# Pooled attention and top-1 experts on one core: a second block of the first expert between attention and the expert loop

## The chip, the cores and the metric

The kernel runs on one core of one Trainium2 chip. The metric is device time in microseconds (us), the median of several runs of one program. Engines are named as in the profile: PE (matrix multiply), PEld (its weight loads), DVE (vector), ACT (scalar), POOL (GpSimd), SP (queue of DMAs). `PEq`, `SPq` and the like are the engines' sequencers.

## The reference

```python
# attention, batch 8, heads 8, seq 576, head_dim 64: keys and values are means over 8 rows
scores = scale * np.matmul(q, k_p.transpose(0, 1, 3, 2))
attn = softmax(scores);  x = (attn @ v_p) as [4608, 512]
# experts: 8, each 512 -> 1024 -> 512; each token goes to the one with the largest logit
logits = x @ w_gate
expert_idx = np.argmax(logits, axis=1)
gate_w = softmax(logits)[np.arange(N), expert_idx]
for e in range(E):
    h = np.maximum(x_sorted[lo:hi] @ w1[e], 0.0)
    y_sorted[lo:hi] = h @ w2[e]
return gate_w[:, None] * y
```

How many tokens an expert gets depends on the data. With the inputs that the reference draws first, the experts 0 to 7 get 1018, 55, 333, 239, 827, 724, 24 and 1388 of the 4608 tokens. Of the first 2304 tokens (batches 0 to 3), 1016 go to expert 0.

## The kernel before

**Attention** runs over 36 units of 128 tokens. Units form seven groups (`bounds`, sizes 6, 6, 6, 6, 6, 4, 2). At the end of a group `route` finds each token's expert and its place among that expert's tokens, and POOL scatters the rows (`scatter`, one indirect DMA per unit) into the DRAM tensor `xs`, which has one segment per expert. Small steps of a route (`fillers`) are spread over later units; what belongs to unit 28, 29 and so on is put there by `put`.

**An early block.** Expert 0 is computed first, in blocks of 256 tokens (`BLK`). After group 2, `early_pe` (line 719) counts whether expert 0 has 256 tokens already and sets the flag `okf`. At unit 28 POOL blanks the tile `xg` (`blank_x`), at unit 29 SP loads the first 256 rows of `xs` into it if the flag is set (`early_load`, line 913). At units 30 and 31 the tile is split into a high and a low half-precision part (`split_early`, on POOL) and turned by two DMA transposes (`turn`) into `xT`. Its first three up products (`UPAT`, of eight) run on PE in units 33 to 35.

**A block** is eight up products (`up`, lines 967 to 969: 12 matmuls each), `relu_hi` on ACT and `relu_lo` on DVE for each of four pairs, and the down products (`finish`, line 1039: 12 matmuls for each half of the hidden columns and each of the two tiles of 128 tokens, 48 in all). `take` (ACT) scales a result, `give` (POOL) scatters it to the output. In a half block (at most 128 tokens) the up products have 128 columns and there are 24 down matmuls.

**Between attention and the loop** (lines 1046 to 1234) stand, in program order: the last group's route steps (`front`, `rest`); ups 3 to 7 of the early block, with `counted` (line 1057: count per expert, ranks, padding) behind the fifth up, `ended` (line 1089: end of each expert's blocks, the last rank chain, all pending scatters, three padding scatters, and `table`, 27 small DVE steps that make the loop's table) behind the sixth, and `tables` (line 1140: a PE transpose of the table and a DVE copy) behind the eighth; then the four `relu_lo`; then the early block's 48 downs. Behind them the x tiles of the loop's first blocks are loaded by the table (`load_x`), split and turned.

**The loop** (line 1260 on) runs T times, T read from the table. Iteration t does block t's ups and downs from `xT`; `arrive` (DVE) copies the next block's transposed tile from `xTs` to `xT`, `split_x` splits the one after it, `trans` sends it through the DMA transpose, `load_x` loads the one after that. In an expert's first block `part` splits the next expert's weights (ACT and DVE), and `wwhole` then loads whole experts' weights, two at the first iteration. Each engine works in program order; SP's queue issues its DMAs in program order too.

Of the kernel before, what the change touches and what calls it, by code (L numbers as in the profile page):

```python
# [32 lines left out]
def kernel(  # L33
# [171 lines left out]
    for e in range(E):  # L205
# [15 lines left out]
    xg, xg2 = (VB[i].rearrange("p y c s x -> p (y c s x)").bitcast(F32)[:, 0:2 * XW]  # L221
               .rearrange("p (j x) -> p j x", j=2) for i in (2, 0))
# [388 lines left out]
    def route(gidx):  # L611
# [107 lines left out]
        def early_pe():  # L719
            pm = psA.tile([128, 512], F32, name="pq", bufs=2)  # L720
            nc.tensor.matmul(pm[:, 0:1], ones, Z["c16"][:, 0:1], start=True, stop=True)
            V.tensor_scalar(okf, pm[:, 0:1], 256.0, None, op0=OP.is_ge)
# [190 lines left out]
    def early_load():  # L913
        assert KVS.pop("early") and not any(g < EARLY for g, _, _ in pend)
        KVS["ok"] = nc.values_load(oki[0:1, 0:1], engines=[ENG.SP], min_val=0, max_val=1)
        with tc.If(KVS["ok"] > 0):
            ld = nc.sync.dma_start(xg, xs[0:BLK, :].rearrange("(j p) x -> p j x", p=128))
        for o in scat[bounds[EARLY][0]:]:
            tc.declare_no_dep(ld.ins, o.ins, reason="rows of other tokens")
        soon.append(ld)  # L920

    put(28, "sp", blank_x, xg)
    put(29, "sp", early_load)
# [123 lines left out]
    rest = [f for _, _, f in fillers]  # L1047
    for x in range(max(len(front), len(rest))):
# [97 lines left out]
    for f in range(FC):  # L1146
        if f >= len(UPAT):
            up(0, f, BLK)
        if f + 1 == 5:
            counted()  # L1150
        if f + 1 == 6:
            ended()
        if f + 1 == 8:
            tables()
        if f in (1, 3):
            relu_hi(f // 2)
    for k in (2, 3):
        relu_hi(k)
    for k in range(4):
        relu_lo(k)  # L1160
    views = [x.rearrange("p a b c -> p (a b c)") for x in qt] + [x.rearrange("p c x -> p (c x)")[:, 0:2048] for x in kv[1:]]
    views = [x.bitcast(F16) for x in views]
    W1[1] = [x.rearrange("p (c f) -> p c f", c=DC) for x in views[:2]]
    W2[1] = [x.rearrange("p (c f) -> p c f", c=FC) for x in views[2:]]
    pY.append(psA.tile([128, 512], F32, name="pq", bufs=2))
    for j, half in ((1, 0), (1, 1), (0, 0), (0, 1)):
        finish(0, j, half)
# [26 lines left out]
    xh2 = kv[1].rearrange("p c x -> p (c x)")[:, 0:1024].bitcast(F16).rearrange("p (j a x) -> p j a x", j=2, a=2)  # L1194
    blank_x(xg2)
    load_x(0)
    load_x(1, xg2)
    wlate(1)
    for j in range(2):
        x, h, l = row(xg[:, j:j + 1]), col(xh[:, j:j + 1, 0]), col(xh[:, j:j + 1, 1])  # L1200
        nc.scalar.activation(h, x, AF.Copy)
# [113 lines left out]
```

## Time and profile before

| | us |
|---|---|
| Median of 3 runs | 645.25 |
| Lowest and highest | 642.09, 645.43 |
| The profiled execution's own time | 646.38 |
| Its span, first to last instruction | 644.4 |
| PE busy | 579.3 |

The profiled execution has 2.0 us around its span. Attention ends near 200 us, the loop's first up product starts at 228.70 us and the last instruction of PE ends near 636 us. PE idles little in the loop; rows with an idle time in brackets show where it does.

### The profile page before, as it was taken

The page shows a single profiled execution, that of the slowest core. Times are in us where ns is not written, and L with a number is a line of the kernel's source. Part 1 is how long each engine was busy: PE and PEld are TensorE (multiplying, and loading weights), DVE is VectorE, ACT ScalarE, POOL GpSimd, SP SyncE. Part 2 cuts the span into 40 slices and gives each one's busy share as a digit, 9 for nine tenths or more (in the row PEclk, how much of TensorE's full clock was granted, in tenths as well). Part 3 has the DMA queues.
Part 4 walks back from the last instruction along what each step waited for, and adds up shares of the span by engine and source line. Part 5 has one row for each costly group of instructions (what it writes and reads, how often), then busy time and mean ns, then how long its engine had stood idle before and what let it go on. Part 6 is the DMA issues. An engine that isn't in the chain of part 4 may idle for free. (4 is left out here: it accounts for less than half of the span.)

```text
span 644.4 us, 15871 instructions
## 1 busy us (share of the span) xinstructions
PE 579.3 (90%) x4694; PEld 422.3 (66%) x4695; DVE 316.9 (49%) x619; ACT 286.8 (45%) x635; POOL 276.4 (43%) x532
## 2 busy tenths in 40 slices
PE   6888898787977698998899999999999989999994
PEld 5777788676865275675566667766667666677662
DVE  7577678886675417221773755122722262221212
ACT  2576688677651226222672753122722352221222
POOL 6799689998684323112314123222121232012212
PEclk9798999899899699999899999999999989999998
DMA  8997789858476565963689497533231333213200
GB/s 244 290 287 222 231 231 311 266 176 248 168 214 232 192 120 152 384 164 85 168 247 327 108 321 251 153 102 77 42 81 53 96 72 102 49 57 79 65 16 30
DMA packets 104203, 108.15 MB, mean 168 GB/s; under 512 B 62310, under 2 KB 72550, under 8 KB 104168
## 3 DMA queue, kind: packets, MB, share of 16 engines
q1 hardware_dynamic: 97528, 86.72, 47.9%
q0 software_dynamic: 6640, 20.99, 8.8%
q8 instruction: 19, 0.31, 0.2%
q14 instruction: 16, 0.13, 0.1%
HBM read 72.99 MB, written 23.37 MB: 150 GB/s over the span
## 5 line engine op out<-in xcount | busy, mean ns | idle before, releaser
L1039 PEld LDWEIGHTS <-bd 128*128 128x128 f16 x936 | 91.6, 99 | 110.1 <-issue 3.6
L1224 POOL TENSOR_TENSOR spacer<-ql,iG 1x1 f32<-1x1 f32 x44 | 23.8, 540 | 218.9 <-ACT ql L1220 218.0
L1033 DVE SCALAR_TENSOR_TENSOR bd<-ps,bd 128x512 f16<-128x512 f32 x44 | 30.2, 690 | 151.3 <-ACT bd L1029 149.5
L1033 DVE SCALAR_TENSOR_TENSOR bd<-pp,bd 128x512 f16<-128x512 f32 x44 | 30.3, 691 | 100.7 <-ACT bd L1029 100.7
L513 ACT ACTIVATE both<-ps,nmx 128x72 f32<-128x72 f32 x288 | 69.0, 330 | 23.9 <-DVE nmx L506 23.3
L1029 ACT ACTIVATE bd<-pp 128x512 f16<-128x512 f32 x44 | 26.2, 597 | 116.8 <-PE pp L969 74.3
L1039 PE MATMUL po<-w,bd 128*128 128x512 f16 x264 | 59.1, 379 | 0.8 <-ACT bd L1029 0.8
L1029 ACT ACTIVATE bd<-ps 128x512 f16<-128x512 f32 x44 | 26.1, 597 | 74.8 <-PE L967 46.1
L1039 PE MATMUL po<-kv,bd 128*128 128x512 f16 x264 | 58.9, 379 | 0.3 <-ACT bd L1029 0.3
L1225 POOL DMA_INDIRECT out_dram<-ql,iG x44 | 43.8, 995 | 21.5 <-issue 20.2
L496 PE MATMUL ps<-bd,qT 128*128 128x144 f32 x256 | 47.0, 310 | 3.5 <-DMA bd<-bd 1.9
L967 PE MATMUL ps<-kv,qt 128*128 128x256 f16 (+1 forms) x176 | 45.7, 267 | 4.9 <-issue 3.2
L1039 PE MATMUL pq<-kv,bd 128*128 128x512 f16 x216 | 48.1, 379 | 0.0
L969 PE MATMUL ps<-kv,qt 128*128 128x256 f16 (+1 forms) x176 | 45.6, 267 | 1.9 <-DVE qt L118 1.9
L967 PE MATMUL ps<-kv,w 128*128 128x256 f16 (+1 forms) x176 | 43.8, 262 | 3.1 <-DVE kv L118 2.8
L969 PE MATMUL ps<-kv,w 128*128 128x256 f16 (+1 forms) x176 | 43.8, 262 | 2.5 <-DVE w L118 2.5
L968 PE MATMUL ps<-kv,qt 128*128 128x256 f16 (+1 forms) x176 | 45.7, 267 | 0.0
L1039 PE MATMUL pq<-w,bd 128*128 128x512 f16 x192 | 45.3, 395 | 0.3 <-remote 0.3
L554 PE MATMUL po<-vb,ph 128*128 128x146 f16 (+2 forms) x384 | 33.4, 234 | 12.6 <-DMA vb<-vc 7.0
L969 PE MATMUL pp<-kv,qt 128*128 128x256 f16 (+1 forms) x176 | 44.7, 263 | 0.0
L968 PE MATMUL pp<-kv,qt 128*128 128x256 f16 (+1 forms) x176 | 44.7, 263 | 0.0
L967 PE MATMUL pp<-kv,qt 128*128 128x256 f16 (+1 forms) x176 | 44.7, 263 | 0.0
(236 smaller groups left out, 1335.8 us busy)
## 6 DMA issues: line engine op xcount, KB each, us to landing
both<-in_moe_w_dram SPq DMA_DIRECT2D x6, 2048.0 KB, 11.7
st<-in_moe_w_dram SPq DMA_DIRECT2D x6, 2048.0 KB
vb<-x_by_expert SPq DMA_DIRECT2D x17, 578.0 KB
st<-in_moe_w_dram SPq DMA_DIRECT2D x8, 1024.0 KB
kv<-in_k_dram SPq DMA_DIRECT2D x7, 1024.0 KB
kv<-in_v_dram SPq DMA_DIRECT2D x7, 1024.0 KB
qt<-in_q_dram SPq DMA_DIRECT2D x6, 1024.0 KB
qt<-in_q_dram SPq DMA_DIRECT2D x4, 512.0 KB
```

Of the source, the lines that this page charges most:

```text
L496: nc.tensor.matmul(ps[:, x * 2 * KP:(x + 1) * 2 * KP], t[:, h, :], BD[b % 3][:, :, h, :], start=True, stop=True)
L513: nc.scalar.activation(p[:, h * KP:(h + 1) * KP], ps[:, x * KP:(x + 1) * KP], AF.Exp, bias=nmx[:, x:x + 1], scale=-1.0)
L554: nc.tensor.matmul(po[:, half, cols], a[:, c * 128:(c + 1) * 128], VB[b % 3][:, y, c, sl, 0:CW], start=st, stop=False, skip_group_check=True)
L967: nc.tensor.matmul(dst, wh, xT[:, d, 0:n], start=(d == 0), stop=False)
L968: nc.tensor.matmul(dst, wh, xT[:, DC + d, 0:n], start=False, stop=False)
L969: nc.tensor.matmul(dst, wl, xT[:, d, 0:n], start=False, stop=(d == DC - 1))
L1029: nc.scalar.activation(hT[0][:, 2 * k:2 * k + 2, :].rearrange("p f t -> p (f t)"), pH[k], AF.Relu)
L1033: V.scalar_tensor_tensor(l, pH[k], 0.0, h, op0=OP.max, op1=OP.subtract)
L1039: nc.tensor.matmul(y, hT[x][:, f, 128 * j:128 * j + 128], W2[s][z][:, f, :], start=(half == x == z == f == 0), stop=(half == z == 1 and f ...
L1224: nc.gpsimd.tensor_tensor(spacer[:, 0:1], ys[j][0:1, 0:1], iG[0:1, j:j + 1].bitcast(F32), op=OP.add)
L1225: st = nc.gpsimd.indirect_dma_start(out=out, out_offset=bass.IndirectOffsetOnAxis(ap=iG[:, j:j + 1], axis=0), in_=ys[j], in_offset=None, b ...
```

## The change

The second block of expert 0 is also computed between attention and the loop. `early_pe` sets the flag to 1 or 2 (256 or 512 tokens); the second early load fills a second tile `xg2`, which now lies in `kv[1]`, as does its split copy `xh2`, and is blanked at unit 28 as well. The loop then has as many blocks fewer as the flag says. `relu_hi(0)` and `relu_lo(0)` go ahead of the last group's route steps, the other relus follow their ups; `counted` stands behind the sixth up; the second tile's split and transpose and then `ended` stand behind the eighth; the first block's downs come in the order of tiles 0, 1; `arrive` for the second block stands among them, and `tables` behind them. Then come the second block's ups, relus and downs, with the loads, splits and transposes for the loop's first two blocks between them.

```diff
@@ -218,8 +218,10 @@
     hT = [x.rearrange("p (f t) -> p f t", f=FC) for x in bd[0:2]]
     xh = bd[2].rearrange("p (j a x) -> p j a x", j=2, a=2)
     ys = [x.rearrange("p h d -> p (h d)") for x in ql]
-    xg, xg2 = (VB[i].rearrange("p y c s x -> p (y c s x)").bitcast(F32)[:, 0:2 * XW]
-               .rearrange("p (j x) -> p j x", j=2) for i in (2, 0))
+    xg, xg2 = (x.rearrange("p (j x) -> p j x", j=2)
+               for x in (VB[2].rearrange("p y c s x -> p (y c s x)").bitcast(F32)[:, 0:2 * XW],
+                         kv[1].rearrange("p c x -> p (c x)")[:, 1024:1024 + 2 * XW]))
+    xh2 = kv[1].rearrange("p c x -> p (c x)")[:, 0:1024].bitcast(F16).rearrange("p (j a x) -> p j a x", j=2, a=2)
 
     def blank_x(x):
         nc.gpsimd.memset(x, 0.0)
@@ -719,7 +721,8 @@
         def early_pe():
             pm = psA.tile([128, 512], F32, name="pq", bufs=2)
             nc.tensor.matmul(pm[:, 0:1], ones, Z["c16"][:, 0:1], start=True, stop=True)
-            V.tensor_scalar(okf, pm[:, 0:1], 256.0, None, op0=OP.is_ge)
+            V.tensor_scalar(okf, pm[:, 0:1], float(BLK), None, op0=OP.is_ge)
+            V.scalar_tensor_tensor(okf, pm[:, 0:1], 2.0 * BLK, okf, op0=OP.is_ge, op1=OP.add)
 
         def early_int():
             V.tensor_copy(oki, okf[0:1, :])
@@ -912,14 +915,16 @@
 
     def early_load():
         assert KVS.pop("early") and not any(g < EARLY for g, _, _ in pend)
-        KVS["ok"] = nc.values_load(oki[0:1, 0:1], engines=[ENG.SP], min_val=0, max_val=1)
-        with tc.If(KVS["ok"] > 0):
-            ld = nc.sync.dma_start(xg, xs[0:BLK, :].rearrange("(j p) x -> p j x", p=128))
-        for o in scat[bounds[EARLY][0]:]:
-            tc.declare_no_dep(ld.ins, o.ins, reason="rows of other tokens")
-        soon.append(ld)
+        ok = nc.values_load(oki[0:1, 0:1], engines=[ENG.SP], min_val=0, max_val=2)
+        for n, x in enumerate((xg, xg2)):
+            with tc.If(ok > n):
+                ld = nc.sync.dma_start(x, xs[n * BLK:(n + 1) * BLK, :].rearrange("(j p) x -> p j x", p=128))
+            for o in scat[bounds[EARLY][0]:]:
+                tc.declare_no_dep(ld.ins, o.ins, reason="rows of other tokens")
+            soon.append(ld)
 
     put(28, "sp", blank_x, xg)
+    put(28, "sp", blank_x, xg2)
     put(29, "sp", early_load)
 
     def first_block():
@@ -1045,6 +1050,8 @@
     pH += [pp[:, 0:512], pp[:, 512:1024]]
     pY = [psA.tile([128, 2, 512], F32, name="po")[:, 0, :]]
     rest = [f for _, _, f in fillers]
+    relu_hi(0)
+    relu_lo(0)
     for x in range(max(len(front), len(rest))):
         for f in (front[x:x + 1] + rest[x:x + 1]):
             f()
@@ -1146,25 +1153,30 @@
     for f in range(FC):
         if f >= len(UPAT):
             up(0, f, BLK)
-        if f + 1 == 5:
+        if f == 3:
+            relu_hi(1)
+            relu_lo(1)
+        if f == 5:
             counted()
-        if f + 1 == 6:
-            ended()
-        if f + 1 == 8:
-            tables()
-        if f in (1, 3):
-            relu_hi(f // 2)
     for k in (2, 3):
         relu_hi(k)
-    for k in range(4):
         relu_lo(k)
+    split_x(xg2, xh2)
+    keep_ids(xg2)
+    move_ids()
+    trans(xh2)
+    ended()
     views = [x.rearrange("p a b c -> p (a b c)") for x in qt] + [x.rearrange("p c x -> p (c x)")[:, 0:2048] for x in kv[1:]]
     views = [x.bitcast(F16) for x in views]
     W1[1] = [x.rearrange("p (c f) -> p c f", c=DC) for x in views[:2]]
     W2[1] = [x.rearrange("p (c f) -> p c f", c=FC) for x in views[2:]]
+    finish(0, 0, 0)
+    finish(0, 0, 1)
     pY.append(psA.tile([128, 512], F32, name="pq", bufs=2))
-    for j, half in ((1, 0), (1, 1), (0, 0), (0, 1)):
-        finish(0, j, half)
+    finish(0, 1, 0)
+    arrive()
+    finish(0, 1, 1)
+    tables()
 
     def entry(kind, t, engines, lo, hi):
         ap = tabs[kind:kind + 1, t:t + 1] if isinstance(t, int) else tabs[kind:kind + 1, ds(t, 1)]
@@ -1190,29 +1202,6 @@
                 part(64, 64, x[64:128, 0])
                 with tc.If(many > 1):
                     part(128, 64, x[0:64, 1])
-
-    xh2 = kv[1].rearrange("p c x -> p (c x)")[:, 0:1024].bitcast(F16).rearrange("p (j a x) -> p j a x", j=2, a=2)
-    blank_x(xg2)
-    load_x(0)
-    load_x(1, xg2)
-    wlate(1)
-    for j in range(2):
-        x, h, l = row(xg[:, j:j + 1]), col(xh[:, j:j + 1, 0]), col(xh[:, j:j + 1, 1])
-        nc.scalar.activation(h, x, AF.Copy)
-        V.tensor_tensor(l, x, h, op=OP.subtract)
-    keep_ids()
-    move_ids()
-    turn()
-    load_x(2)
-    split_x(xg2, xh2)
-    keep_ids(xg2)
-    trans(xh2)
-    with tc.If(nc.values_load(tab[0:1, 1:2], engines=[ENG.Activation, ENG.DVE, ENG.SP], min_val=0, max_val=1) > 0):
-        for j in range(8):
-            wsplit(1, j)
-        wwhole(2, 1)
-        wwhole(3, 0)
-    T = nc.values_load(tab[0:1, 0:1], min_val=1, max_val=TMAX)
 
     given = []
 
@@ -1229,10 +1218,42 @@
             tc.declare_no_dep(st.ins, o.ins, reason="rows of other tokens")
         given.append(st)
 
+    take(0)
     take(1)
     give(1)
+    give(0)
+    take_ids()
+    load_x(0)
+    load_x(1, xg2)
+    for h in range(2):
+        for f in range(4 * h, 4 * h + 4):
+            up(0, f, BLK)
+        for k in (2 * h, 2 * h + 1):
+            relu_hi(k)
+            relu_lo(k)
+    split_x()
+    keep_ids()
+    move_ids()
+    trans()
+    for half in range(2):
+        finish(0, 1, half)
+    arrive()
+    load_x(2)
+    split_x(xg2, xh2)
+    keep_ids(xg2)
+    trans(xh2)
+    take(1)
+    give(1)
+    for half in range(2):
+        finish(0, 0, half)
     take(0)
     give(0)
+    with tc.If(nc.values_load(tab[0:1, 1:2], engines=[ENG.Activation, ENG.DVE, ENG.SP], min_val=0, max_val=2) > 0):
+        for j in range(8):
+            wsplit(1, j)
+        wwhole(2, 1)
+        wwhole(3, 0)
+    T = nc.values_load(tab[0:1, 0:1], min_val=1, max_val=TMAX)
 
     def part(s, en):
         with tc.If(en > 0):
```

## Rows read from the trace of the kernel before

**Rows 1.** The page, busy time by engine: each engine's busy time, share of the span and instructions.

```profile
PE 579.3 (90%) x4694; PEld 422.3 (66%) x4695; DVE 316.9 (49%) x619; ACT 286.8 (45%) x635; POOL 276.4 (43%) x532
```

**Rows 2.** Busy time in stretches around the hand-over from attention to the loop (all of core 0): the stretch, its length, busy us of each engine with its instructions, the clock granted to TensorE as a share of full speed, the DMA share, GB/s.

```profile
207.82:214.81 6.99, 0.01 (x2) 0.03 (x1) 3.05 (x27) 0.00 (x0) 6.06 (x11) 0.69 0.77 290
214.81:223.40 8.59, 8.26 (x26) 3.19 (x27) 3.88 (x7) 2.24 (x4) 0.38 (x3) 0.66 0.44 142
228.70:239.18 10.48, 10.48 (x96) 9.40 (x97) 1.38 (x2) 1.81 (x3) 2.80 (x11) 1.00 0.88 160
239.19:249.70 10.51, 10.51 (x50) 4.61 (x47) 8.63 (x9) 9.27 (x11) 0.20 (x1) 1.00 0.29 54
249.70:252.52 2.82, 0.01 (x1) 0.03 (x1) 2.82 (x4) 1.67 (x3) 1.58 (x1) 1.00 0.27 61
252.52:273.35 20.83, 20.83 (x144) 14.10 (x145) 5.25 (x7) 4.10 (x6) 5.92 (x16) 1.00 0.99 370
```

**Rows 3.** The timeline of PE at the hand-over: start us, us, engine, line, operation, out<-in, count, and in brackets the idle time before it and what ended it.

```profile
199.54 0.27 PE L967 MATMUL ps<-kv,w 128*128 128x256 f16 x1
...
203.42 0.18 PE L1059 MATMUL pq<-c,ones 128*128 128x8 f16 x1 [1.10 <-DVE c L1052]
...
204.84 0.34 PE L1093 MATMUL pq<-lt,ones 128*128 128x8 f16 x8
...
214.81 0.37 PE L1142 MATMUL pq<-ident,tf 128*8 128x128 f32 x1 [6.99 <-DVE tab L1138]
215.51 7.89 PE L1039 MATMUL pq<-w,bd 128*128 128x512 f16 x24 [0.33 <-remote]
...
228.70 0.28 PE L967 MATMUL ps<-kv,w 128*128 128x256 f16 x1
```

**Rows 4.** The groups of instructions with shapes apart, first of the three lines of the up product into PSUM tile ps: the operands (the name after the comma is the up weights' tile: w for slot 0, which the even experts use, qt for slot 1), the shape, the count, busy us and mean ns. A full block (256 tokens) has 16 such instructions of 128x256, a half block (128 tokens) 16 of 128x128.

```profile
L967 PE MATMUL ps<-kv,qt 128*128 128x256 f16 x144 | 40.0, 278 | 2.3 <-DVEq L1238 0.8 <-ACT qt L116 0.8 <-issue 0.7
...
L967 PE MATMUL ps<-kv,w 128*128 128x256 f16 x128 | 35.6, 278 | 3.1 <-DVE kv L118 2.8 <-DVE bd L899 0.2
...
L967 PE MATMUL ps<-kv,w 128*128 128x128 f16 x48 | 8.2, 219 | 0.0
...
L967 PE MATMUL ps<-kv,qt 128*128 128x128 f16 x32 | 5.7, 219 | 2.5 <-issue 2.5
```

**Rows 5.** The timeline of DVE at the hand-over, columns as in group 3: the first and the last of the last group's rank chain, the first and the last instruction of the table, then one `relu_lo`, one `arrive` and one low half of `split_x` from the loop's first block.

```profile
204.45 0.17 DVE L674 TENSOR_TENSOR rt<-pq,roh 128x16 f32<-128x16 f32 x1
...
205.97 0.17 DVE L697 RECIPROCAL both<-res 128x2 f32<-128x2 f32 x1
209.00 0.22 DVE L1112 TENSOR_SCALAR tf<-pq,tv 128x1 f32<-128x1 f32 x1 [2.85 <-PE pp L969]
...
213.49 0.14 DVE L1138 TENSOR_TENSOR tab<-pq,okf 1x1 int32<-1x1 f32 x1
...
240.25 0.69 DVE L1033 SCALAR_TENSOR_TENSOR bd<-pp,bd 128x512 f16<-128x512 f32 x1 [4.55 <-ACT bd L1029]
...
242.37 0.68 DVE L910 COPY kv<-kv 128x2048 f16<-128x2048 f16 x1
242.97 1.22 DVE L899 TENSOR_TENSOR bd<-vb,bd 128x1024 f16<-128x1024 f32 x1
```

**Rows 6.** The timeline of POOL at the hand-over, columns as in group 3: the first and the last of the six row scatters that are pending at the end of attention (three more, of padding, follow them).

```profile
202.42 0.97 POOL L702 DMA_INDIRECT x_by_expert<-both,rpos  x1 [7.10 <-DVE pq L640]
...
208.80 0.97 POOL L702 DMA_INDIRECT x_by_expert<-both,rpos  x1 [0.21 <-issue]
```

**Rows 7.** The timeline near the end of attention, columns as in group 3: POOL's blank of the first early x tile, SP's early load and the eight moves behind it and the transposes of the first block, then PE where it waits for the last move, and the first early up.

```profile
168.83 1.09 POOL L225 MEMSET vb<- 128x1156 f32 x1
...
171.70 0.37 SPq L917 DMA_DIRECT2D vb<-x_by_expert  x1
172.31 7.80 SPq L1014 DMA_DIRECT2D vb<-vc  x8
180.59 2.77 SPq L903 DMA_TRANSPOSE kv<-bd  x2
...
181.44 0.58 PE L554 MATMUL po<-vb,ph 128*128 128x73 f16 x7 [0.66 <-DMA vb<-vc]
...
187.15 0.27 PE L967 MATMUL ps<-kv,w 128*128 128x256 f16 x1
```

**Rows 8.** The timeline of SP's queue at the start of the loop, columns as in group 3: the two loads of x tiles as soon as the table is there, and the first transpose that the loop waits for.

```profile
217.64 2.81 SPq L1179 DMA_DIRECT2D vb<-x_by_expert  x2
...
228.86 4.02 SPq L906 DMA_TRANSPOSE kv<-kv  x1
```

**Rows 9.** DMA issues with their median time from issue to landing: first two rows over the whole execution, then two of the stretch 252 to 276 us, in which the next two experts' weights are loaded.

```profile
out_dram<-ql,iG POOLq DMA_INDIRECT x44, 3.0
...
kv<-bd SPq DMA_TRANSPOSE x23, 4.3
...
out_dram<-ql,iG POOLq DMA_INDIRECT x4, 7.2
kv<-bd SPq DMA_TRANSPOSE x1, 13.9
```

**Rows 10.** Where the loop first enters the body for half blocks of slot 1: PE's timeline, columns as in group 3, and the instruction queue in the stretch 293 to 298 us (packets, MB, share of 16 engines).

```profile
296.81 0.22 PE L967 MATMUL ps<-kv,qt 128*128 128x128 f16 x1 [2.45 <-issue]
...
q8 instruction: 1, 0.02, 1.1%
```

## The prediction

> **What bounds the kernel now.** I read the busy times first [rows 1]: PE is busy for 579.3 of 644.4 us. So I asked where PE is not busy, by stretches and by its timeline around the hand-over from attention to the loop. In the loop a full block takes PE 20.83 us and fills it: 10.48 us of ups and, from the difference, 10.35 us of downs, at the full clock [rows 2]. The loop is bound by PE; a block taken out of it is worth 20.83 us, and the same block put anywhere else costs 20.83 us of PE again. The change can win only where PE idles or is clocked low. The hand-over is such a place: PE's last up ends at 207.82 us, and it then waits 6.99 us for the end of `table` on DVE, only to transpose it [rows 3]; in that stretch PE is busy for 0.01 us [rows 2]. The downs behind it start at a granted clock of 0.66 on the mean of 8.59 us [rows 2], after the idle stretch, so that 48 of them take 228.70 - 215.51 = 13.19 us [rows 3] where the loop needs 10.35: 2.84 us lost.
>
> **Does the block leave the loop?** Only if the flag is 2, that is, if expert 0 has 512 of the first 2304 tokens. Counting the reference's argmax on the inputs as drawn gives 1016. The trace agrees with these inputs: 16 first-line ups make a block, so 144 + 128 instructions of 128x256 are 9 + 8 = 17 full blocks, and 48 + 32 of 128x128 are 3 + 2 = 5 half ones [rows 4]; the counts per expert give 4 full blocks for expert 0, and 17 full and 5 half in all. So T falls from 21 to 20, and the block that goes is a full one. The loop from its first up to the end of the span is 644.40 - 228.70 = 415.70 us before; one block less makes 394.87. The 2.82 us behind the first iteration, where PE waits for the split of the next expert's weights [rows 2], stays: that iteration keeps this work.
>
> **PE's new order, and the sum.** I start at 199.54, the fourth up, the same instruction in both kernels [rows 3].
> - Three ups at 10.48 / 8 = 1.31: 3.93.
> - Wait for the count. Before, PE waits 1.10 behind two ups [rows 3]. One more up stands ahead now (1.31 less waiting), but `relu_lo(0)`, 0.69 [rows 5], stands ahead of the DVE chain that makes the count's operand: 1.10 - 1.31 + 0.69 = 0.48.
> - Count, ranks and the eight small matmuls of `ended`: from the trace some 0.1 behind 203.42 and 0.2 behind 204.84 [rows 3]: 0.31. Their operand `lt` is on DVE by then.
> - Two ups, 2.62; the first block's downs at once, 10.35; the transpose of the table, 0.37 [rows 3], which now finds the table done.
> - The second block: 20.83.
>
> That is 38.89, so the loop starts at 238.43, and the span is 238.43 + 394.87 = 633.30: 11.10 us less, as the place lost 6.99 + 2.84 + 0.33 and part of the 1.10. This is the sum without any new wait.
>
> **What is added beside PE, and what hides it.**
> *Second early load and blank.* POOL's second blank, 1.09 and a small one [rows 7], stands ahead of the split of the first block and so of the transposes at 180.59. SP's second load stands ahead of the eight moves that PE waits for at 181.44, after which it was idle; the first load and its branch hold SP from 171.70 to 172.31, 0.61 us [rows 7]. Nothing hides that: the moves are issued one behind the other, and the last of them ends PE's wait. The first transposes start at 180.59 and the first early up at 187.15 [rows 7], 6.56 later; with 4.3 to landing and two of them issued in 2.77, the 1.2 us of POOL about uses up what is left over. The bounds are 0 (other engines set the pace after it) and 2.0 us (0.61, the 1.2 of POOL, and a wider branch); I take 0.8, nearest to the SP row.
> *The chain to the second block's `xT`.* All in DVE's order behind the eighth up, in the sum without shift at 206.9: `relu_hi(3)` on ACT (taken as 0.7, like the `relu_lo` of 0.69), the split's high half on ACT (taken as 1.2, like the low half) and its low half, 1.22, which ends near 210; then the rank chain, 205.97 + 0.17 - 204.45 = 1.69, the table, 213.49 + 0.14 - 209.00 = 4.63, and the copy `arrive`, 0.68 [rows 5]: 217.0. PE is done with the first downs and the table's transpose at 217.6. The slack is 0.6 us; a table that took as long as before hides just under the 10.35 us of downs, and without that cover it would cost the 6.99 again. The transpose has from 210 to 216.3 to land, 6.3 us, against a median of 4.3 [rows 9].
> *POOL.* `keep_ids(xg2)` waits for the split's end and stands ahead of the pending scatters, so these start near 210.5 and not at 202.42; six at (208.80 - 202.42) / 5 = 1.28 [rows 6] end at 218.2, with 3.0 to landing 221 (estimate by the other indirect DMA, [rows 9]). The loads of the loop's first tiles wait for them and for the table at 218: issued near 221, as 217.64 before [rows 8], landed by 225, and their first reader, `split_x`, comes behind the second block's ups at 228.1. 3 us of slack: no cost.
> *The transpose for the loop's first block* goes out near 231 and is needed at 238.4: 7.4 less 0.68 for the copy against 4.3 to landing, or some 6.3 where the issue itself takes 4.02 and not 2 [rows 8]. No cost. The flag's extra DVE step, the moved waits for the table's registers and `give` lie beside PE's work.
> I take 0.3 for the `xT` chain (0 to 2) and 0.5 for what the shorter run of expert 0 does to the next expert's start (0 to 3.4, third rival). Gain: 11.10 - 0.8 - 0.3 - 0.5 = 9.5 us. The profiled execution's own time, 646.38, becomes 636.9; it stands 1.1 above the median of the three runs, and the forecast for the median is 645.25 - 9.5 = 635.8.
>
> **A rule against it, twice.** The loads of two experts' weights make a transpose land after 13.9 us and an output scatter after 7.2 in place of 3.0 [rows 9]. The Trainium skill, "DMA: Bandwidth & Descriptors", section "Issuing engines are not separate DMA queues", says that DMAs from any engine end on the same 16 DMA engines and interleave. By that rule the new transpose, which now runs beside POOL's scatters, is late (second rival), and the rows above agree that traffic stretches it. At the first entry of the half body of slot 1 PE waits 2.45 us for nothing the profile shows, and one packet of the instruction queue falls into that stretch [rows 10]. The Trainium skill, "Runtime: NRT & Kernel Launch", section "Instruction fetch mechanics", says that a taken branch out of the fetched window has to fetch its code by DMA. By that rule the third rival is real.
>
> **The rivals.**
> 1. *Forecast*: PE runs through, 635.8. For it: every chain above fits under PE's work. Against it: the slack of the `xT` chain is under 1 us.
> 2. *The second block's transpose is late.* From a landing over 6.3 us PE waits at 217.6. At 9 it costs 2.7: 638.5. At the 13.9 of the weight loads [rows 9] it costs 7.6 and the low clock again, 2.84: no gain is left, 645 to 646. Against it: the scatters' stretch has a DMA share of 0.77 [rows 2], weight loads fill it.
> 3. *The next expert's start.* One block less lies between the loads of 8 MB of weights in the first iteration and expert 1's half block, which PE reaches 2 x 20.83 + 2.82 = 44.5 us after the loop's start in place of 65.3. The transposes and x loads queued behind the weights, and the entry of [rows 10], then fall into their end. If the 2.45 stretches as the output scatters do, 7.2 / 3.0 = 2.4 times, it costs 3.4: 638.7.
> 4. *The flag comes out as 1, not 2* (the change doesn't do what it says). Then the extra block works on a blank tile and the loop keeps 21 blocks: the loop starts at 238.43 + 1.6 in place of 228.70, 11.3 us slower: 656.6. It decides from the 512th token of expert 0 among the first 2304; 1016 speak against it.
>
> **How the numbers follow.** Chances: 1 has 0.66, 2 has 0.13 (most of it near 638.5), 3 has 0.14, 4 has 0.03, and 0.04 is for a long stall that I don't see, within or past 645. The range takes in the sum without new waits less what the runs scatter (645.25 - 11.1 = 634.2, lowest run 3.2 below its median; I go to 632.8) and, above, the attention tail at 2.0, 1.8 of `xT` and 3.4 of rival 3 together: 645.25 - 3.9 = 641.3; I go to 641.0. About 0.5%, 3.2 us, is what a measurement of this kernel can tell from no change. Faster than 642.0 are case 1, nearly all of 3 and most of 2: 0.88; within it the rest of 2 and of the last: 0.08; slower 0.04.
>
> **What would show it.** Right: PE without an idle gap over 1 us from the fourth up to the loop, its clock at 1.00 throughout, the 48 first downs in some 10.4 us, 20 `arrive` copies within the loop, the loop's first up near 239 to 240 us, and the span near 635. Wrong: a wait of PE for DVE's `arrive` before the second block's ups (rival 2), a wait over 3 us ahead of the 128x128 ups of slot 1 (rival 3), 21 loop blocks still (rival 4), or an attention that ends more than 2 us later.

## The result, and the profile after

The changed kernel is slower, not faster: 646.46 us median over 20 runs (642.8 to 651.7) against 644.21 over 20 runs of the kernel before on the same chip, ratio 1.0063, 95% interval [1.0038, 1.0088]. The ratio, here and below, leaves out the runs in a slower state that some executions fall into, so it is not the quotient of the medians, which is 1.0035 here. The forecast was a gain of 9.5 us. The profiled execution's own time is 645.5, its span 643.5; before these were 646.38 and 644.4. PE's work is the same, and its busy time rose by 3.6 us, which is the first sign of a lower clock in places. The page's busy time by engine:

```profile
PE 582.9 (91%) x4694; PEld 427.6 (66%) x4695; DVE 321.3 (50%) x620; ACT 286.0 (44%) x634; POOL 276.0 (43%) x532
```

The block did leave the loop. PE's timeline of the changed kernel at the hand-over (start us, us, engine, line, operation, out<-in, count, idle before it and what ended it), the rows that answer to [rows 3]: the fourth up, the matmuls behind the eighth, the first downs, the table's transpose, the second block's first up, the loop's first up, and last the half body's first entry, which answers to [rows 10]:

```profile
200.97 0.27 PE L972 MATMUL ps<-kv,w 128*128 128x256 f16 x1
...
208.10 0.34 PE L1100 MATMUL pq<-lt,ones 128*128 128x8 f16 x8
208.31 1.02 PE L1044 MATMUL po<-w,bd 128*128 128x512 f16 x4
...
222.06 0.27 PE L1149 MATMUL pq<-ident,tf 128*8 128x128 f32 x1 [3.23 <-DVE tab L1145]
222.57 0.35 PE L972 MATMUL ps<-kv,w 128*128 128x256 f16 x1 [0.24 <-DVE kv L913]
...
246.52 0.28 PE L972 MATMUL ps<-kv,w 128*128 128x256 f16 x1 [1.28 <-ACTq L1286]
...
297.66 0.24 PE L972 MATMUL ps<-kv,qt 128*128 128x128 f16 x1 [4.62 <-issue]
```

The first downs went as forecast: right behind the ups, done in 222.06 - 3.23 - 208.31 = 10.5 us. Then come three waits that the sum did not have: 3.23 for a table that is still late, 1.28 at the loop's entry where there was next to none before, and 4.62 at the half body's entry where it was 2.45 [rows 10]. The loop's first up comes at 246.52, not 238.43. The busy times by stretch (stretch, length, PE, PEld, DVE, ACT, POOL with their instructions, TensorE's granted clock, DMA share, GB/s) answer to [rows 2]:

```profile
208.31:222.06 13.75, 10.52 (x54) 4.63 (x51) 6.47 (x38) 3.51 (x5) 7.88 (x18) 1.00 0.64 189
222.06:234.50 12.44, 12.20 (x96) 10.10 (x97) 1.96 (x4) 1.19 (x2) 6.83 (x16) 0.86 0.78 234
234.50:246.52 12.02, 10.74 (x53) 4.80 (x50) 4.44 (x5) 4.47 (x6) 1.35 (x8) 1.00 0.29 59
246.52:270.37 23.85, 21.01 (x144) 13.95 (x145) 12.87 (x14) 12.11 (x15) 5.37 (x13) 1.00 0.38 92
```

The idle time ahead of the table's transpose is again followed by a lower granted clock: 0.86 on the mean of the second block's ups, which take some 12 us instead of 10.48.

**Why the table is late.** DVE's timeline of the changed kernel, from the second block's split through the last group's rank chain to the table's end (answers to [rows 5]):

```profile
211.24 1.23 DVE L902 TENSOR_TENSOR kv<-kv 128x1024 f16<-128x1024 f32 x1 [0.26 <-ACT kv L901]
212.38 0.17 DVE L676 TENSOR_TENSOR rt<-pq,roh 128x16 f32<-128x16 f32 x1
212.65 0.17 DVE L679 TENSOR_REDUCE rpf<-rt 128x2 f32<-128x16 f32 x1
218.22 0.17 DVE L696 CAST rpos<-rpf 128x2 int32<-128x2 f32 x1 [5.39 <-DMA x_by_expert<-both,rpos]
...
221.78 0.14 DVE L1145 TENSOR_TENSOR tab<-pq,okf 1x1 int32<-1x1 f32 x1
221.84 0.67 DVE L913 COPY kv<-kv 128x2048 f16<-128x2048 f16 x1
```

The chain stops in its third instruction. The cast writes the tile of positions `rpos`, which comes from a pool of two buffers; the one it gets was that of the last full group of six units, and the scatters of that group read it. They were expected to be long done. POOL's timeline shows why one was not (answers to [rows 6]):

```profile
197.30 0.97 POOL L704 DMA_INDIRECT x_by_expert<-both,rpos  x1 [0.22 <-issue]
198.29 0.20 POOL L881 TENSOR_TENSOR gC<-kv,zf 128x2 f32<-128x2 f32 x1
198.44 0.20 POOL L882 TENSOR_TENSOR iC<-kv,zi 128x2 int32<-128x2 int32 x1
212.61 0.20 POOL L886 TENSOR_TENSOR kv<-far,zi 128x2 int32<-128x2 int32 x1 [13.97 <-DVE rt L676]
...
213.38 0.98 POOL L704 DMA_INDIRECT x_by_expert<-both,rpos  x1 [0.26 <-issue]
```

Five of the six scatters are out by 198.3. The sixth stands in POOL's queue behind `keep_ids(xg2)`, whose last step overwrites the identity column of the second block's x tile and so has to wait 13.97 us until DVE has read that tile in the split (the split ends at 212.47; the row names the instruction right behind it). The sixth scatter goes out at 213.38, lands some 4.8 us later, and only then DVE may cast the positions. The table, which the prediction had done at 217.0 - 0.68 = 216.3 (217.8 on this execution's clock, whose fourth up is 1.43 later), is done at 221.92.

**Why the loop is entered late.** ACT's last scaling of outputs, `take(0)`, now belongs to the second block and runs behind its downs; ACT's arrival at the loop stands behind it, and so does the branch on the table with the loading of the loop's count, which the change put last:

```profile
240.23 0.69 ACT L1209 ACTIVATE ql<-pq,gB 128x512 f32<-128x512 f32 x1 [1.46 <-POOL iC L882]
245.27 0.69 ACT L1209 ACTIVATE ql<-po,gB 128x512 f32<-128x512 f32 x1 [4.36 <-PE po L1044]
```

PE's downs end at 245.24, the scaling at 245.96, and PE enters at 246.52.

**Why the half body is entered late.** SP's timeline: the loads of two experts' weights in the loop's first turn (8 MB), and the transpose behind them.

```profile
268.61 3.30 SPq L89 DMA_DIRECT2D both<-in_moe_w_dram  x2
272.76 6.42 SPq L89 DMA_DIRECT2D st<-in_moe_w_dram  x2
287.67 8.88 SPq L909 DMA_TRANSPOSE kv<-bd  x1
```

Before, the same loads were issued at 251.37 and 254.86. They belong to the loop's first turn, behind that turn's transpose; the first turn was the second block and is now the third, so they slid by 17 us on the clock, and by some 20 against the blocks. Two stretches ahead of the entry, columns as in the stretches above, show that they now reach it:

```profile
288.00:293.00 5.00, 5.00 (x24) 2.06 (x22) 0.00 (x0) 0.69 (x1) 1.38 (x3) 1.00 1.04 392
293.00:298.00 5.00, 0.38 (x4) 0.23 (x3) 0.00 (x0) 0.69 (x1) 1.81 (x6) 0.97 1.20 215
```

In the kernel before the DMA engines were idle at 286 to 290 us; here they are full (shares over 1 are overlapping packets) until PE starts. The packet of the instruction queue that belongs to the entry starts at 294.64, 1.6 us after PE went idle; before, it started at 294.12, 0.2 us ahead of PE's idle time. From the packet's start to PE's it is 2.6 to 3.1 us in all the traces of this text; where the wait is longer, it is the packet that starts later.

### The profile page after: what moved, and what is told of

Same layout as the page of the kernel before. It is cut to its first block, busy times and chain, and to the rows that moved or that the text cites. A ratio compares the mean times of both kernels' runs of the same rounds, so it can differ in the third digit from the quotient of the medians.

```text
span 643.5 us, 15731 instructions
## 1 busy us (share of the span) xinstructions
PE 582.9 (91%) x4694; PEld 427.6 (66%) x4695; DVE 321.3 (50%) x620; ACT 286.0 (44%) x634; POOL 276.0 (43%) x532
## 5 line engine op out<-in xcount | busy, mean ns | idle before, releaser
L972 PE MATMUL ps<-kv,qt 128*128 128x256 f16 (+1 forms) x176 | 46.4, 270 | 6.4 <-issue 5.2
L972 PE MATMUL ps<-kv,w 128*128 128x256 f16 (+1 forms) x176 | 45.5, 272 | 4.5 <-DVE kv L118 2.8
L974 PE MATMUL ps<-kv,qt 128*128 128x256 f16 (+1 forms) x176 | 46.4, 270 | 1.8 <-DVE qt L118 1.8
L974 PE MATMUL ps<-kv,w 128*128 128x256 f16 (+1 forms) x176 | 45.4, 271 | 2.5 <-DVE w L118 2.5
L973 PE MATMUL ps<-kv,qt 128*128 128x256 f16 (+1 forms) x176 | 46.6, 271 | 0.0
L973 PE MATMUL ps<-kv,w 128*128 128x256 f16 (+1 forms) x176 | 45.4, 271 | 0.0
```

The source lines that it names most:

```text
L972: nc.tensor.matmul(dst, wh, xT[:, d, 0:n], start=(d == 0), stop=False)
L973: nc.tensor.matmul(dst, wh, xT[:, DC + d, 0:n], start=False, stop=False)
L974: nc.tensor.matmul(dst, wl, xT[:, d, 0:n], start=False, stop=(d == DC - 1))
```

## The experiments

My theory after the first reading: three costs, the held-up scatter (some 5 us with the clock), the loop's entry (about 1) and the slid weight loads (about 2), hide a gain of the forecast's size. The rival: the changed kernel starts and ends its attention later (its second load), and the hand-over is worth little. For all kernels one table, from PE's timelines: the fourth up's start, from there to the first up of expert 0's fourth block (the same instruction in all of them, behind one loop turn with the split of the next expert's weights), and from there to the end of the span. The forecast had 73.82 - 11.10 + 0.3 = 63.0 in the middle and 371.5 behind it.

| kernel | fourth up | to fourth block | to the end | own span | median of runs | ratio, 95% |
|---|---|---|---|---|---|---|
| before | 199.54 | 73.82 | 371.04 | 644.4 | | |
| changed | 200.97 | 69.40 | 373.13 | 643.5 | 646.46 | 1.0063 [1.0038, 1.0088] |
| e1 scatters first | 206.80 | 65.27 | 374.33 | 646.4 | 648.65 | 0.9969 [0.9933, 1.0006] |
| e2 positions three deep | 203.59 | 72.70 | 374.51 | 650.8 | 652.22 | 1.0045 [1.0012, 1.0077] |
| e3 second load alone | 201.82 | 74.28 | 371.40 | 647.5 | 652.00 | 1.0019 [0.9987, 1.0052] |
| e4 changed, again | 204.71 | 71.75 | 374.44 | 650.9 | 654.11 | 1.0052 [1.0011, 1.0093] |
| e5 before, again | 204.46 | 72.52 | 371.02 | 648.0 | 651.66 | 0.9988 [0.9963, 1.0013] |
| e6 = e1 + entry ahead | 208.12 | 64.73 | 377.35 | 650.2 | 647.07 | 0.9913 [0.9880, 0.9945] |
| e7 = e6 + weights ahead | 203.07 | 65.57 | 371.26 | 639.9 | 645.55 | 0.9893 [0.9862, 0.9923] |
| e8 = e7 + load behind moves | 203.67 | 64.73 | 371.50 | 639.9 | 642.91 | 0.9862 [0.9828, 0.9897] |
| e9 table alone | 201.88 | 78.14 | 367.98 | 648.0 | 649.82 | 1.0101 [1.0074, 1.0129] |
| e10 = e8 - scatters first | 201.59 | 68.54 | 371.57 | 641.7 | 642.45 | 0.9984 [0.9946, 1.0022] |
| e11 = e8, again | 203.35 | 64.61 | 371.14 | 639.1 | 637.92 | 0.9897 [0.9843, 0.9951] |

The kernel before had medians of 650.6 beside e1 to e4, 651.76 beside e5 to e8 and 643.2 beside e9 to e11, each group on a chip of its own; the ratios are against these runs. They differ from the quotients of the medians by up to 0.2%: those are 1.0025 for e2, 0.9928 for e6 and 0.9918 for e11.

**e1, scatters first.** The changed kernel with the identity copies behind the pending scatters:

```
     split_x(xg2, xh2)
-    keep_ids(xg2)
-    move_ids()
     trans(xh2)
     ended()
+    keep_ids(xg2)
+    move_ids()
```

> The changed kernel with one move: POOL's keep_ids and move_ids for the second block stand behind ended, so that the pending scatters no longer wait behind them for DVE's split. Theory (the last group's cast of positions is the third writer of a tile two deep and waits 5.39 us for the scatters of two groups before, the last of which stands behind keep_ids): that wait on DVE goes, the table is done before the first block's downs end, the 3.23 us wait of PE ahead of the table's transpose and the low clock behind it (some 1.9 us over the second block's ups) go: about 5 us faster than the changed kernel. Rival (the new DMA transpose lands late beside POOL's scatters): the scatters now start near 206 us and run beside the transpose, so xT comes later, PE waits for arrive instead, and little or nothing is won.

DVE's cast and PE's transpose of the table in e1:

```profile
220.97 0.17 DVE L696 CAST rpos<-rpf 128x2 int32<-128x2 f32 x1 [0.16 <-DVE rpf L679]
...
225.78 0.27 PE L1149 MATMUL pq<-ident,tf 128*8 128x128 f32 x1
```

The wait of 5.39 is 0.16, PE's wait for the table is gone, and the second block's ups run at the full clock. Against e4, the changed kernel on the same chip, the median is 5.5 us lower (5.1 without e4's longest run of 659.75), and the middle column 6.5. Two waits stay: 1.30 at the loop's entry, 4.18 at the half body's.

**e2, positions three deep.** The other way to free the cast: the order stays, `rpos` gets a third buffer.

```
-            Z[n] = work.tile(shape, dt, name="r" + n)
+            Z[n] = work.tile(shape, dt, name="r" + n, bufs=3 if n == "pos" else 2)
```

> The changed kernel with the tile of positions three deep, and nothing moved: the scatters stay late on POOL. Theory: the DVE wait of 5.39 us goes alone, and PE's 3.23 us wait and the low clock with it, about 5 us faster than the changed kernel; the loads of the loop's first x tiles stay late, with slack. Rival (the wait is for the DMA rings, or the transposes are what is late): DVE waits as before, at the cast or at arrive, and the time stays.

DVE's cast in e2:

```profile
215.47 0.17 DVE L696 CAST rpos<-rpf 128x2 int32<-128x2 f32 x1
```

The cast waits for nothing, and PE's wait for the table went too (the transpose at 221.28 has none), which shows that the tile's two buffers are what holds the cast. But the time did not follow: 1.0045 against 1.0052 for the changed kernel on the same chip (e4). PE's timeline in e2, the second block's ups:

```profile
221.28 0.27 PE L1149 MATMUL pq<-ident,tf 128*8 128x128 f32 x1
...
227.43 0.27 PE L973 MATMUL ps<-kv,w 128*128 128x256 f16 x1 [1.05 <-issue]
...
228.84 0.27 PE L974 MATMUL ps<-kv,w 128*128 128x256 f16 x1 [1.14 <-issue]
...
230.27 0.27 PE L972 MATMUL ps<-kv,w 128*128 128x256 f16 x1 [1.16 <-issue]
```

With three shorter ones (0.45, 0.45, 0.33) these sum to 4.58 us in which PE waits for nothing that the profile shows, in code without a branch, and the clock falls to 0.56 on the mean of 232 to 238 us. The late scatters and the loads of x tiles run in that stretch (DMA share 0.75 in 226 to 232), and one instruction packet falls into 218 to 236. PE's code coming late would be one reason, but the trace speaks against it: that packet starts at 222.57, 1.2 us behind the block's first up (1.4 in e11, 1.5 in e1), and is over at 223.70, ahead of the first stall. What PE waits for stays open; no other kernel with the early second block has one over 0.5 us between the fourth up and the loop.

**e3, second load alone.** The kernel before with only the second blank and the second early load into the new tile, the block itself left in the loop.

> The kernel before with the second early load and the second blank at unit 28 alone; the second tile's rows are not used, the loop loads them again. By the prediction's step: 0.8 us slower than before (0 to 2). Theory: the end of attention has slack behind it, since in the changed kernel the fourth up comes earlier against attention's middle than before, so within 1 us of before. Rival (the eight moves behind the load let PE idle long enough for its clock to fall to half near 181 to 188 us, as in the changed kernel's trace, and this is what costs): 2 to 5 us slower than before.

1.0019, its interval from under 1 to 1.0052: the load costs at most 0.5%, 3.4 us, which does not tell the theory from the rival. Its trace has the table's wait at 6.97 as before, and the half body's entry at 2.84.

**e4, the changed kernel again**, for a reference on the chip of e1 to e3.

> The changed kernel itself, for its time on this chip beside the others and a second trace. Theory: the waits of the first trace come again: 5 us on DVE's cast of positions, about 3 on PE ahead of the table's transpose, over 1 at the loop's entry, and 4 to 5 at the first entry of the half body of slot 1 against 2.45 before. Rival (chance of one execution): some of them are gone.

1.0052, with the same three waits: 5.02 for the table, 1.29 at the loop, 4.40 at the half body.

**e5, the kernel before again.** It is the test of the rival's start: in four traces of changed kernels the reciprocal of the fourth unit stood at 48.6 to 50.0 us, in those of before and of e3 at 45.7 and 44.2.

> The kernel before, unchanged, timed against itself. Theory: the changed kernels lose time in the hand-over and in the loop, not in the attention; if their longer start (the reciprocal of the fourth unit at 48.6 to 50.0 us in four traces of kernels that have the change, 44.2 to 45.7 in two that do not) is chance, this trace may show it anywhere between 44 and 50, and the ratio is 1.000 within 0.004. Rival: the start belongs to the change; then this trace shows 44 to 46 us, and the first of the early ups at 187 to 190 us.

DVE's row of that reciprocal's first step, in e5:

```profile
49.45 0.15 DVE L584 TENSOR_SCALAR ri<-po 128x8 f32<-128x8 f32 x1
```

49.45 in the kernel before, and 45.67 and 45.97 in e7 and e8, which have the change: the early or late start belongs to the execution. That rival falls, and a single profiled span can't be compared across kernels by less than 4 us.

**e6, entry ahead.** e1, and the branch on the table and the loop's count moved ahead of the second block's outputs:

```
     trans(xh2)
+    with tc.If(nc.values_load(tab[0:1, 1:2], engines=[ENG.Activation, ENG.DVE, ENG.SP], min_val=0, max_val=2) > 0):
...
+    T = nc.values_load(tab[0:1, 0:1], min_val=1, max_val=TMAX)
     take(1)
     give(1)
...
     give(0)
-    with tc.If(nc.values_load(tab[0:1, 1:2], engines=[ENG.Activation, ENG.DVE, ENG.SP], min_val=0, max_val=2) > 0):
...
-    T = nc.values_load(tab[0:1, 0:1], min_val=1, max_val=TMAX)
```

> The changed kernel with the scatters first and with the branch on the table and the loading of the loop's count placed ahead of the second block's outputs, as the kernel before has them ahead of its own. Theory: the 1.28 us that TensorE waits for ScalarE at the loop's entry falls to 0.7 to 0.9, since the last scaling of outputs (0.69 us) still ends there but no register is loaded behind it; against the kernel before 0.996, against the scatters-first kernel half a microsecond, too little to be told by time. Rival: the wait is the last scaling and the entry itself; it stays at 1.28.

The loop's entry waits 0.86 instead of 1.28, and now on DVE's arrival. The half body's entry was worse in this execution, and its time (652.0) the longest of its six runs:

```profile
290.50:295.50 5.00, 5.00 (x24) 2.06 (x21) 0.00 (x0) 0.69 (x1) 1.38 (x3) 1.00 1.04 393
295.50:302.37 6.87, 0.02 (x2) 0.03 (x2) 0.00 (x0) 0.69 (x1) 1.81 (x6) 0.69 1.33 181
```

PE stands 6.85 us with the DMA engines full throughout. The ratio, 0.9913, was lower than the 0.996 expected; its interval overlaps that of e1.

**e7, weights ahead.** e6, and half of the loop's first weight loads issued ahead of the loop:

```
     trans(xh2)
+    wwhole(2, 1)
     with tc.If(nc.values_load(tab[0:1, 1:2], engines=[ENG.Activation, ENG.DVE, ENG.SP], min_val=0, max_val=2) > 0):
...
-        wwhole(2, 1)
         wwhole(3, 0)
...
-        V.scalar_tensor_tensor(n3[:, 2:3], ex_, 0.0, head, op0=OP.is_equal, op1=OP.mult)
-        V.scalar_tensor_tensor(tf[:, 7:8], n3[:, 2:3], 2.0, tf[:, 7:8], op0=OP.mult, op1=OP.add)
```

> The kernel of e6 with the third expert's whole weights (4 MB of the 8 MB that the loop's first turn loads) issued ahead of the loop, and the term of the table that asks for them in the first turn taken out. Theory: a block out of the loop has put the loop's loads of weights one block later, into the first entry of the second slot's half body; with half of them gone earlier they end by 286 us and the wait at that entry falls from 4.2 to 4.6 us to 2.5 to 2.9, so some 2 us less than e6 in the trace and 0.993 against the kernel before. Rival: the entry's length has nothing to do with the weights (the code's place, or TensorE's own fetch); it stays at 4.2 or above.

The two stretches ahead of the entry and PE's entry in e7:

```profile
284.00:289.00 5.00, 5.00 (x25) 2.24 (x23) 0.11 (x1) 0.69 (x1) 1.38 (x3) 1.00 0.72 158
289.00:292.62 3.62, 0.64 (x3) 0.13 (x2) 0.00 (x0) 0.69 (x1) 1.36 (x4) 1.00 0.30 80
```

```profile
292.62 0.22 PE L972 MATMUL ps<-kv,qt 128*128 128x128 f16 x1 [2.98 <-issue]
```

The wait is 2.98 (2.53 in e8, 2.42 in e10, 2.62 in e11) against 4.18 to 6.85 in the five traces in which the loads end there, and 2.35 to 2.84 in the four that keep the block in the loop. The last column of the table goes back to 371; of the 6.1 us between e6 and e7 this wait is 3.9, and 1.7 is a clock in the fourth block that falls in some traces only (see the terms of the sum below). In the middle column the edit may cost something: PE's wait behind the loop's first block, for the split of expert 1's weights, is 3.70 in e7, 4.37 in e10 and 3.85 in e11, where it is 2.77 to 2.87 in the other kernels with the early second block (2.83 in e8).

**e8, second load behind.** e7, and the second early load behind the attention's last eight moves instead of ahead of them:

```
-        for n, x in enumerate((xg, xg2)):
-            with tc.If(ok > n):
...
+        one_load(0, xg)
...
     put(29, "sp", early_load)
+    put(30, "act2", one_load, 1, xg2)
```

> The kernel of e7 with the second early load issued behind the attention's last eight moves instead of ahead of them. Theory: those moves stand 0.6 us behind the first load, as in the kernel before, instead of 1.6; TensorE waits some 1 us less for them at 180 to 190 us, and its granted clock falls there later or for a shorter time; 1 to 2 us less than e7, 0.991 against the kernel before. Rival: the moves are bound by what they copy, not by their place on the queue; the waits and the time stay as in e7 within 0.5 us.

The moves stand 0.63 behind the first load, as before. 0.9862 against e7's 0.9893, with intervals that overlap. PE's waits for the moves sum to 2.0 us against 2.8, but the clock still falls to 0.50 at 184 to 188 us, and the first early up comes 13.1 us behind the reciprocal of the thirty-first unit, 12.5 in e7. In e11, the same program, the clock stays at 1.00 in that stretch, and PE waits 2.59 us for the first block's transpose instead. Whether this edit is worth 2 us or nothing is open.

**e9, table alone.** The kernel before with the count behind the sixth up, the rank and table chain behind the ups and the transpose behind the first downs; no early second block.

> The kernel before with the count behind the sixth up, the rest of the rank and table chain behind the ups, and the table transposed behind the first block's downs; no early second block, the loop's count as before. Theory: TensorE no longer waits 6.97 us for the table, but the second block's rows are still asked for through the table, and the loop's first up stood 13.9 us behind the table's transpose; with the transpose now at about 218 us (on the clock of rows whose fourth up starts at 199.54) the first up comes at about 232 instead of 228.7: the wait moves to the loop's entry, where it is some 13 us, and the time is 1.005 of the kernel before (1.000 to 1.009). Rival: the table's wait was a cost by itself; 5 us or more are saved (0.992 or less).

PE's timeline in e9, the table's transpose and the loop's first up:

```profile
221.72 0.27 PE L1142 MATMUL pq<-ident,tf 128*8 128x128 f32 x1
233.78 0.37 PE L967 MATMUL ps<-kv,w 128*128 128x256 f16 x1 [11.79 <-DMA kv<-bd]
```

1.0101, above the 1.009 that the theory allowed: the 6.97 us are not saved but moved, and grow to 11.79, since the second block's rows are still asked for through the table. Moving the table behind the downs pays only because the early second block needs no table.

**e10 and e11, all the edits without and with e1's order**, on one chip.

> The kernel of e8 with GpSimd's identity copies of the second block put back ahead of the sixth scatter of the last full group, as the change has them. Theory: the position's cast waits for that scatter again, the table is 3 to 5 us late, and the time lies 4 to 6 us above that of e8 (0.993 against the kernel before, if e8 gives 0.986). Rival: with the loop's two waits mended the order on GpSimd no longer decides; within 1.5 us of e8.

> The kernel of e8 once more, on the chip of e9 and e10. Theory: 0.986 of the kernel before (0.983 to 0.990 by its first interval), TensorE without a wait over 1 us between the fourth up and the loop, 2.5 to 3.0 us at the half body's first entry. Rival: the first one gained from early starts of the attention (46 us at the fourth unit against 49 to 50 in other traces); with a start at 49 us or later it shows 0.993 or more.

DVE's cast in e10 and in e11:

```profile
218.59 0.19 DVE L696 CAST rpos<-rpf 128x2 int32<-128x2 f32 x1 [5.15 <-DMA x_by_expert<-both,rpos]
```

```profile
215.42 0.17 DVE L696 CAST rpos<-rpf 128x2 int32<-128x2 f32 x1 [0.16 <-DVE rpf L679]
```

The medians are 642.45 and 637.92: 4.5 us for the place of five small copies on POOL's queue, in the middle column 3.9. e11 has PE without a wait over 1 us from the fourth up to the loop, an entry of 0.90, the half body at 2.62, and 0.9897 of the kernel before; its attention started at 46.38 in the profiled execution, so the rival of that expectation isn't tested by it.

## Why the prediction was wrong

**Right.** PE bounds the kernel, and the hand-over is where it idled. The flag is 2 and the block left the loop (rival 4 false). The first downs run right behind the ups in 10.5 us at a granted clock of 1.00, as the sum had them. Rival 2 is false, though not by the changed kernel's trace, in which the transpose of 212.49 had landed only because the table was late. In the six traces in which it was not (e1, e2, e6, e7, e8, e11) `arrive` waits 0.21 to 0.73 us for the transpose, 4.3 to 5.0 us behind its issue where the forecast allowed 6.3, and PE waits for neither. The size of the gain was right for a kernel without these waits, which takes edits that the forecast did not have: e8 and e11 have 64.7 and 64.6 us from the fourth up to the fourth block against a forecast of 63.0, and ran at 0.9862 and 0.9897 where 635.8 / 645.25 is 0.9853.

**The step that failed** is the chain to `xT` with the one on POOL beside it. I took the rank chain at the 1.69 us that it had in the trace of before, and of POOL I wrote that the scatters start later by `keep_ids(xg2)` and that this costs nothing, because I followed the scatters only to the readers of the rows they write. I did not follow them to the next writer of what they read. The chain's cast writes a tile of two buffers, and the moved copies hold a scatter of two groups back: 5.39 us on DVE, 3.23 (5.02 in e4) on PE, then some 1.6 of low clock in the second block. The runs price the order on POOL's queue at 5.1 to 5.5 us (e4 to e1) and 4.5 (e10 to e11). That the cast's wait is all of this is not shown: e2 takes that wait away alone and gains nothing, with stalls of 4.58 us in its trace that no run explains. I had named the 6.99 us as what is lost if the cover is gone; it was gone by another wait than the one I looked for.

**Terms of the sum that were mis-sized.** The next expert's start, taken at 0.5 with an upper end of 3.4, is the last column against 371.03: 2.1 us in the changed kernel, 3.3 in e1, 3.4 in e4 and 6.3 in e6. Two costs stand in it. One is the half body's entry, 4.18 to 6.85 us instead of 2.35 to 2.84: rival 3 is true, and it was not a bad case but the ordinary one. The mechanism was as that rival has it: one block less, 20.83 us, lies between the loads and the half block, and this is the 20 us by which the loads now come later against the blocks. The other cost the sum did not have. The fourth block's first 3 us, in the changed kernel and in the kernel before (columns as in the stretches above):

```profile
270.37:273.37 3.00, 3.00 (x15) 2.08 (x16) 0.71 (x1) 0.00 (x0) 2.18 (x5) 0.51 0.91 279
273.35:276.35 3.00, 3.00 (x29) 2.69 (x28) 0.00 (x0) 0.70 (x2) 1.22 (x3) 1.00 1.04 397
```

From this block's first up to the idle time ahead of the half body it is 22.67 us in the changed kernel, e1, e4 and e6, and 21.0 in the kernel before, e2, e7 and e8: 1.66 us of low clock behind the 2.84 us wait for the split of expert 1's weights. The kernel before has that wait too (2.81) and its clock stays at 1.00 behind it [rows 2]; e10 (23.59) and e11 (22.38) have the low clock although the weight loads are out of the way. Why it falls in some traces and not in others stays open. The two costs sum to 3.8 us in the changed kernel, where the column rose by 2.1: further on in the loop some of it comes back, which no run explains.

By the Trainium skill, "Runtime: NRT & Kernel Launch", section "Instruction fetch mechanics", a taken branch to code outside the fetched window has to wait for a DMA that fetches it. The traces agree, in that one instruction packet falls into the stretch ahead of the entry in every one of them, PE starts 2.6 to 3.1 us behind its start, and the wait goes from 2.4 to 3.0 us at DMA shares of 0.24 to 0.37 during it to 4.2 to 6.9 at shares of 1.17 to 1.39.

The loop's entry was taken at nothing ("the moved waits for the table's registers and `give` lie beside PE's work"); it is 1.28, of which e6 shows 0.4 to be the registers' place. The attention's end was taken at 0.8 with 2.0 as upper end: the fourth up stands at 202.0 on the mean of the two traces of the kernel before and at 202.8 in the two of the changed one, but single starts scatter by 4 to 5 us, so the traces carry no finer figure; e3's ratio bounds it. Counted from DVE's reciprocal of the thirty-first unit, which leaves the early or late start out, the fourth up comes 21.6 to 24.5 us later (mean 23.0) in the three traces without the second load (before, e5, e9) and 22.6 to 26.1 (mean 24.7) in the seven with it ahead of the moves: 1.7 us, nearer the term's upper end than the 0.8, but not clear of this scatter.

**The account.** On the mean of the two traces each, the changed kernel reaches the fourth up 0.8 later, gains 73.17 - 70.58 = 2.6 in the hand-over in place of 11, and loses 2.8 behind it: +1.0 us. The runs say +2.2 and +3.5 by medians, +4.1 and +3.4 by the ratios. The rest, 1 to 3 us, lies within the scatter of the single traces' starts; no run pins it down.

## What to carry to other kernels

Before an instruction with a wait is moved ahead on a queue, list what stands behind it there, and follow each of those not only to the readers of what it writes but to the next writer of what it reads: with two buffers, the tile written two rounds later waits for it. A block that is taken out of a loop takes a turn's worth of prefetches with it; what the first turn issued comes a turn later against the work, and meets what comes next unless it is issued ahead of the loop, as half of it was in e7. And a wait that is covered must be ended by something that no longer needs it: moving the table alone made 6.97 us into 11.79, moving it with an early second block and an unblocked queue gave 0.3% (e1, not clear of zero), and 1 to 1.4% with the loop's entry and its weight loads mended too (e8, e11).

## What the runs showed of the hardware

- The first entry of a loop body waited 2.35 to 2.98 us in eight traces with no weight load beside it (DMA shares of 0.24 to 0.37 during the wait), and 4.18 to 6.85 in five in which weight loads filled the DMA engines (1.17 to 1.39). The packet of the instruction queue took 0.9 to 1.2 us in all of them and PE started 2.6 to 3.1 us behind its start; in the eight it started within 0.4 us of PE going idle, in the five 1.4 to 4.1 us after it. What the weight loads delay is the packet's start.
- In e2 PE stood six times for 0.33 to 1.16 us in straight code, for nothing that the profile shows, beside a DMA share of 0.75, with no instruction packet in the stretch of the stalls. What it waited for stays open.
- The same program reached its fourth unit of attention at 45.7 or 49.45 us in two executions. What decides it stays open.
